# First GEMM of blocks 2 to 5: three products by one level as PSUM chains, four by two levels that add to them; the second GEMM in another order

## The chip, the cores and the metric

One Trainium2 chip, one of its cores. The time is device microseconds for one launch. The kernel before takes 632.58 us (median of 3 runs, 631.98 to 633.35). The engines are TensorE (PE in the profile, PEld its weight loads), VectorE (DVE), ScalarE (ACT), GpSimd (POOL) and SyncE (SP), which here issues every transfer.

## The reference

Retention (a linear recurrence over 768 steps with a decay for each head), then a two-layer network with ELU between the layers:

```python
B, H, S, D = 4, 8, 768, 64        # 3072 tokens, 512 features
for t in range(S):
    state = gamma[None, :, None, None] * state + np.einsum('bhd,bhe->bhde', k[:, :, t], v[:, :, t])
    y[:, :, t] = scale * np.einsum('bhd,bhde->bhe', q[:, :, t], state)
x = y.transpose(0, 2, 1, 3).reshape(B * S, H * D)
h = x @ w_in                      # 3072x512 @ 512x2048
g = np.where(h > 0.0, h, np.exp(np.minimum(h, 0.0)) - 1.0)
out = g @ w_out                   # 3072x2048 @ 2048x512
```

## The kernel before, in words

Tokens go in six blocks of 512 (`tb` 0 to 5). A block has a first GEMM (x by w_in), an ELU on its 128x8192 result, and a second GEMM (g by w_out). Meanwhile the retention of the next block is computed in pieces (`retention_step`: scores, states, three steps of outputs). Everything is fp32, and everything is kept in the order in which the program issues it: each engine works through its own queue in that order, and waits where an operand isn't there yet.

Both GEMMs are multiplied by Strassen's scheme in Winograd's form: seven products M1 to M7 of quarter matrices in place of eight, with sums before (on the operands) and after (on the results). "Two levels" applies the scheme again inside one of the seven. In blocks 2 to 5:

- First GEMM. M2 and M3 go by two levels (`first_twice`, seven inner products of four matmuls with 128 columns each, L885). The other five go by one level (`first_rest`, L931: for each of four row groups `n` four matmuls with 256 columns). Products that are to be added on the TensorE share a PSUM bank: M1, M6 and M5 of a row group run into the same bank `qa`, M7 and M4 into `qd`, and between them ScalarE copies what stands there so far (`kept`, L704). VectorE adds the pieces that stand in different banks (L899, L939).
- ELU (`elu`, L486): ScalarE computes relu and exp (L491, L492), VectorE closes with one scalar_tensor_tensor (L495), which is queued in a list `later` and issued some steps further on. A block has 16 such tiles of 128x512. They are spread over the first GEMM and the start of the second. After a row group's last tile VectorE forms T3 = C22 - C12 and T1 = C12 - C11 (L944).
- Second GEMM (`second_twice`): seven products in the order `ORDER2` = 1, 2, 6, 7, 5, 3, 4, each by two levels: seven inner products of four 128-column matmuls (L973), 49 in all. For each of the seven VectorE forms four sums of its input (`input_parts`, L847), and twice a new input in C11 (`next_input`, L787). Inner products use three PSUM tags: `pa` (two banks), `pb`, `pd` (one bank each). p1, p6, p5, p3 of a product run into one `pa` bank, p7 and p4 into `pd`, p2 into `pb`; the next of the seven begins before the last two inner products of the one before are done.
- Weights of inner products come from DRAM: `fetch_small` (L809) issues a 256 KB load into a ring of 11 slots (`wq`) whenever a slot comes free.
- Retention: the chunk of q, k and v is loaded (`load`, L110, 1 MB, four for a block), GpSimd scales v by a decay (`scale_v`, L286), and VectorE multiplies the outputs, on their way from PSUM, by powers of the decay in `etab` (L398).
- Blocks 0 and 1 go by one level in the first GEMM (`first`, L758). The second GEMM of block 1 already goes by `second_twice`, and during block 1 the inner sums of w_in for M2 and M3 are formed by VectorE and written to DRAM (`combine_small`, L833; the writes are L657).

Of the kernel before, what the change touches and what calls it, by code (L numbers as in the profile page):

```python
# [18 lines left out]
def kernel(  # L19
# [71 lines left out]
    gq["T1"] = gq["C12"]  # L91
# [197 lines left out]

    rows = lambda n: slice(n * D, (n + 1) * D)  # L290
# [87 lines left out]
    def outputs(tb, pp):  # L378
# [18 lines left out]
        for sub in range(2):  # L397
            nc.vector.tensor_tensor(  # L398
                out=place_of(x_of(tb)[:, :, 2 * pp * C : 2 * (pp + 1) * C])[:, :, :, sub, :], in0=y[sub],
                in1=place_of(powers[:, :, i * C : (i + 2) * C])[:, :, :, sub, :], op=ALU.mult,  # L400
            )
# [344 lines left out]
    def first(n):  # L746
# [18 lines left out]
        def use(name, h):  # L765
            flat = lambda x: x.rearrange("p a b -> p (a b)")
            elu(flat(mine(name)), flat(h))
            if name == "C12":

                sub = lambda o, x, y: nc.vector.tensor_tensor(out=o, in0=x, in1=y, op=ALU.subtract)  # L770
                later.append(lambda: sub(mine("T3"), mine("C22"), mine("C12")))
                later.append(lambda: sub(mine("T1"), mine("C12"), mine("C11")))
# [5 lines left out]
    ORDER2 = [1, 2, 6, 7, 5, 3, 4]  # L778

    INPUT2 = {1: "C11", 2: "C21", 3: "C22", 4: "C11", 5: "T1", 6: "C11", 7: "T3"}  # L780

    def next_input(j):

        x, op = {2: ("T3", ALU.add), 6: ("C21", ALU.subtract)}[j]
        for n in range(NQ):
            q = slice(2 * n, 2 * n + 2)
            nc.vector.tensor_tensor(out=gq["C11"][:, q], in0=gq[x][:, q], in1=gq["C11"][:, q], op=op)  # L787
# [4 lines left out]
    TWICE = [2, 3]  # L792
    SMALL = {5: 0, 6: 1, 7: 2, 3: 3}
    small_w, to_fetch, before = [], [], []
    for tb in range(1, NTB):
        for j in TWICE if tb > 1 else []:
            m1, m2, *mine = [(tb, 0, j, k) for k in (1, 2, 6, 7, 5, 4, 3)]
            to_fetch += [m1] + before[:1] + [m2] + mine[:2] + before[1:] + mine[2:3]
            before = mine[3:]
        to_fetch, before = to_fetch + before, []  # L800
        for j in ORDER2:
            last = (4, 3) if j == 4 and tb == NTB - 1 else (3, 4)
            mine = [(tb, 1, j, k) for k in (1, 2, 6, 7, 5) + last]
            to_fetch += mine[:2] + before + mine[2:5]
            before = mine[5:]
        to_fetch, before = to_fetch + before, []
# [19 lines left out]
    W_IN = {2: w_a_[:, :, :, 1], 3: w_s_[:, :, 2]}  # L826

    def combine_small(j):

        t = stage.tile([P, 4, 4, P], FP32, name="wi", tag="stage")  # L830
# [25 lines left out]
    def combine_x_twice():  # L856

        t = tpool.tile([P, 4, 2, 2, P], FP32, name="ts", tag="ts")
        b = [xb[:, 2 + k].rearrange("p (h t c) -> p t h c", h=2, t=2)[:, u] for k in range(2) for u in range(2)]
        for _ in quarters_of_input(t[:, :, 0], *b):  # L860
            pass
        for n, j in enumerate(TWICE):
            b11, b12, b21, b22 = (x[:, n] for x in b)
            s1, s2, s3, s4 = (t[:, k, 0, n] for k in range(4))
            xs[j] = {1: b11, 2: b21, 3: b22, 4: s4, 5: s1, 6: s2, 7: s3}


    PLACE = {2: "C11", 3: "C12"}

    def first_twice(tb, j):  # L870

        dst = PLACE[j]
        place = lambda name, r, t: gq[name][:, 4 * r : 4 * r + 4, P * t : P * t + P]
        full = lambda t: t.rearrange("p a (b c) -> p (a b) c", c=P)
# [17 lines left out]
        def lift(ps, o=None):  # L892
            if o is None:
                o = full(mpool.tile([P, 2, TH], FP32, name="m", tag="m"))
            nc.scalar.copy(o, ps)
            return o

        def plus(r, t, ps, m):
            nc.vector.tensor_tensor(out=place(dst, r, t), in0=ps, in1=m, op=ALU.add)  # L899

        pa = full(bank("a"))
        product(1, pa, True)
        m1 = lift(pa)
        yield
        pb = full(bank("b"))
        product(2, pb, True)
        plus(0, 0, pb, m1)
        product(6, pa, False)
        u2 = lift(pa)
        pd = full(bank("d"))  # L910
        product(7, pd, True)
        m7 = lift(pd)
        yield
        product(5, pa, False)
        plus(1, 1, pa, m7)
        yield
        product(4, pd, False)
        plus(1, 0, pd, u2)
        yield
        product(3, pa, False)  # L920
        lift(pa, place(dst, 0, 1))

    def first_rest(n, j, ps):
# [3 lines left out]
            4: (w_b[n][:, :, 1], xt[3]), 7: (w_s[n][:, 1], xt[2]),  # L927
        }[j]
        for fi in range(2):
            for j2 in range(2):  # L930
                nc.tensor.matmul(  # L931
                    ps[:, fi, :], lhsT=w[:, fi, j2, :], rhs=x[:, j2, :],
                    start=(j in (1, 7) and fi == 0 and j2 == 0), stop=(j2 == 1), skip_group_check=True,
                )

    def first_end(n, name, ps, x=None):

        g = gq[name][:, 2 * n : 2 * n + 2, :]
        nc.vector.tensor_tensor(out=g, in0=ps, in1=g if x is None else x, op=ALU.add)  # L939
        g = g.rearrange("p a b -> p (a b)")  # L940

        def combine():
            mine = lambda x: gq[x][:, 2 * n : 2 * n + 2, :].rearrange("p a b -> p (a b)")
            sub = lambda o, x, y: nc.vector.tensor_tensor(out=o, in0=x, in1=y, op=ALU.subtract)  # L944
            sub(mine("T3"), mine("C22"), mine("C12"))
            if n < NQ - 1:
                sub(mine("T1"), mine("C12"), mine("C11"))
            else:
                later.append(lambda: sub(mine("T1"), mine("C12"), mine("C11")))

        return lambda: elu(g, g, 3, combine if name == "C22" else None)

    def second_twice(tb, behind_last):
        quarter = lambda x, r, t: x[:, 4 * r : 4 * r + 4, P * t : P * t + P]
        ts, kept2 = {}, {}

        def inputs(j):
            for _ in input_parts(j):
                pass

        def input_parts(j):
            x, t = gq[INPUT2[j]], tpool.tile([P, 4, 4, P], FP32, name="ts", tag="ts")
            b11, b12, b21, b22 = (quarter(x, a, b) for a in range(2) for b in range(2))
            for n, _ in enumerate(quarters_of_input(t, b11, b12, b21, b22)):
                if n == 1:
                    yield
            ts[j] = {1: b11, 2: b21, 3: b22, 4: t[:, 3], 5: t[:, 0], 6: t[:, 1], 7: t[:, 2]}
# [15 lines left out]

        def add(o, x, y):
            nc.vector.tensor_tensor(out=o, in0=x, in1=y, op=ALU.add)  # L985
# [64 lines left out]
        def sum_up(j, m):  # L1050

            kept2[j] = m
            if j == 2:
                add(m, kept2[1], m)
                store("C11", m)
            elif j == 6:
                add(m, kept2[1], m)
            elif j == 5:
                add(m, kept2[6], m)
                h = hpool.tile([P, 512], FP32, name="h", tag="h")  # L1060
# [3 lines left out]
            elif j == 3:  # L1064
                add(m, kept2[5], m)
                store("C12", m)
# [4 lines left out]
        for _ in input_parts(1):  # L1071
            yield "input"
        yield "inputs"
        before = iter(())
        for at, j in enumerate(ORDER2):
# [3 lines left out]
            if j == 1:  # L1079
                yield "tail"  # L1080
            for _ in before:
                pass
            if at:
                yield "first"
            if j == 2:
                flush()
                next_input(2)
            if j == 5:
                next_input(6)
            if j == 1:  # L1090

                next(cur)
                yield "elu"
                next(cur)
            parts = input_parts(ORDER2[at + 1]) if at + 1 < 7 else iter(())
            if j in (2, 5):

                next(parts)
            else:
                for _ in parts:  # L1100
                    pass
            if at == 6:
                behind_last()
            if j != 1:
                next(cur)
                yield "middle"
                next(cur)
            for _ in parts:
                pass
            before = cur  # L1110
            yield j
        for _ in before:
            yield "rest"
# [189 lines left out]
    some(smalls[2], 1)  # L1303
    for n in range(NQ):
# [8 lines left out]
        if n in (1, 2):  # L1313
            some(smalls[n + 1], 1)
        elif n == 3:
            scale_v(2 * CPB, True)
        for _ in tail:
            pass
        for at, s in enumerate(cur):
            next(sides[n], None)  # L1320
# [8 lines left out]
        for _ in sides[n]:  # L1329
            pass  # L1330
        tail = cur
# [10 lines left out]
    sec = second_twice(1, combine_x_twice)  # L1342
    for _ in range(3):
        next(sec)
    next(tail)
    next(tail)
    next(sec)
    for _ in tail:
        pass
    flush()  # L1350
    step, VISITS = 0, [(0, "end"), (2, "middle"), (3, "first"), (4, "end"), (5, "end")]
    for s in sec:
        if s == "first":
            step += 1
        at = (step, s if s in ("first", "middle") else "end")
        if at in VISITS:
            retention_step(2, VISITS.index(at))
        if s == ORDER2[-1]:
            break
    tail = sec  # L1360


    for tb in range(2, NTB):
        more = tb + 1 < NTB
        qa, qd, u2, end = {}, {}, {}, None

        def rest(n, j):
# [143 lines left out]
```

## Time and profile before

| | us |
|---|---|
| median of 3 runs | 632.58 (631.98 to 633.35) |
| profiled execution, span | 631.6 |
| block 2, from its first matmul | 234.2 |
| block 3: first GEMM and retention from 334.12 to 385.75, the rest to 433.50 | 51.6 + 47.8 |
| PE busy / DVE busy / ACT busy / POOL busy | 623.8 / 482.1 / 255.3 / 22.1 |
| mean DMA rate over the span | 214 GB/s |

The span is the time from the first to the last instruction of the one execution that was profiled. "Busy" of PE counts a matmul from its start to its modelled end, and those overlap by some 0.17 us, so what a group of matmuls costs is read from the starts of the groups that follow each other. In a timeline line the first number is the start, the second the duration, and the bracket at the end is the idle time of the engine before it, with what ended that.

### The profile page before, as it was taken

How to read it: one execution, taken by the hardware profiler on the slowest of the kernel's cores; microseconds unless marked ns; L12 is line 12 of the kernel's file. 1: busy time of each engine (PE TensorE's matmuls, PEld its weight loads, DVE VectorE, ACT ScalarE, POOL GpSimd, SP SyncE). 2: the span in 40 equal slices, each digit the busy share in tenths (PEclk: the TensorE clock that was granted, in tenths of full speed). 3: DMA queues.
4: the chain of work that ended last, by engine and by line, in shares of the span. 5: the costliest groups of instructions: out<-in, count | busy, mean ns of one | idle time of the engine just before them, and what ended most of it. 6: DMA issues, size and time to landing. Idle time of an engine off the chain costs nothing.

```text
span 631.6 us, 16140 instructions
## 1 busy us (share of the span) xinstructions
PE 623.8 (99%) x6678; PEld 560.5 (89%) x6678; DVE 482.1 (76%) x882; ACT 255.3 (40%) x476; POOL 22.1 (4%) x30
## 2 busy tenths in 40 slices
PE   8999999999999999999999999999999999999997
PEld 6864578888899999888999989999989999988997
DVE  6688789989799665799585589777489877558975
ACT  6798646025541114553112646112465211366311
POOL 1021000000000000200000100000110000000000
PEclk9999999999999999999999999999999999999999
DMA  8698669699288788306888702889810698700794
GB/s 329 260 416 295 186 202 268 196 272 319 113 266 257 234 258 315 141 2 199 257 258 296 278 2 71 268 280 289 317 64 16 220 310 252 207 17 4 239 309 151
DMA packets 75897, 136.32 MB, mean 216 GB/s; under 512 B 6320, under 2 KB 31792, under 8 KB 70832
## 3 DMA queue, kind: packets, MB, share of 16 engines
q1 hardware_dynamic: 75824, 135.29, 64.9%
q8 instruction: 53, 0.87, 0.5%
q14 instruction: 20, 0.16, 0.1%
HBM read 114.03 MB, written 21.23 MB: 214 GB/s over the span
## 4 chain that ended last, share of the span: by engine, by line
PE 98%; DVE 0%; issue 0%; ACT 0%
PE pa L973 20%; PE pa L931 10%; PE pd L973 10%; PE pb L973 5%; PE pa L885 5%; PE pb L931 4%; PE pa L758 4%; PE pa L535 3%; PE qa L931 3%; PE x L625 3%; PE pd L885 2%; PE qd L931 2%; PE pd L931 2%; PE pd L758 2%; PE pa L625 2%; PE kv L352 2%
## 5 line engine op out<-in xcount | busy, mean ns | idle before, releaser
L981 ACT COPY ms<-pa 128x128 f32<-128x128 f32 x104 | 27.6, 265 | 148.2 <-PE pa L973 148.2
L973 PE MATMUL pa<-ts,wq 128*128 128x128 f32 x560 | 74.2, 275 | 0.0
L973 PE MATMUL pd<-ts,wq 128*128 128x128 f32 x552 | 73.5, 276 | 0.0
L973 PEld LDWEIGHTS pa<-ts,wq 128*128 128x128 f32 x560 | 68.5, 192 | 0.4
L973 PEld LDWEIGHTS pd<-ts,wq 128*128 128x128 f32 x552 | 67.1, 192 | 0.6 <-DVE res L985 0.2
L973 PE MATMUL pa<-gC,wq 128*128 128x128 f32 x480 | 64.6, 278 | 0.0
L492 ACT ACTIVATE r<-r 128x512 f32<-128x512 f32 x96 | 60.5, 631 | 3.1
L973 PEld LDWEIGHTS pa<-gC,wq 128*128 128x128 f32 x480 | 59.0, 192 | 1.3
L491 ACT ACTIVATE r<-gC 128x512 f32<-128x512 f32 x64 | 39.9, 624 | 31.9 <-DVE gC L939 31.9
L985 DVE TENSOR_TENSOR res<-pd,ms 128x128 f32<-128x128 f32 x68 | 19.5, 287 | 39.6 <-PE pd L973 38.4
L495 DVE SCALAR_TENSOR_TENSOR gC<-r,gC 128x512 f32<-128x512 f32 x64 | 42.6, 697 | 0.7 <-ACT r L492 0.7
L847 DVE TENSOR_TENSOR ts<-gC,ts 128x512 f32<-128x512 f32 x60 | 41.3, 688 | 1.0
L847 DVE TENSOR_TENSOR ts<-gC 128x512 f32<-128x512 f32 x60 | 41.0, 683 | 0.0
L286 POOL TENSOR_TENSOR chunk<-chunk,vf 128x512 f32<-128x512 f32 x16 | 19.4, 1212 | 429.6 <-DMA chunk<-in_qkv_dram 429.6
L973 PE MATMUL pb<-gC,wq 128*128 128x128 f32 x240 | 31.7, 275 | 0.0
L1006 ACT COPY res<-pa 128x128 f32<-128x128 f32 x34 | 9.0, 265 | 55.1 <-PE pa L973 55.1
L973 PEld LDWEIGHTS pb<-gC,wq 128*128 128x128 f32 x240 | 29.2, 192 | 0.0
L704 ACT COPY m<-pa 128x512 f32<-128x512 f32 x24 | 14.0, 582 | 33.0 <-PE pa L758 18.7
L939 DVE TENSOR_TENSOR gC<-qa,gC 128x512 f32<-128x512 f32 x8 | 5.5, 692 | 25.0 <-PE qa L931 18.3
L931 PE MATMUL pa<-xt,w_s 128*128 128x256 f32 x96 | 23.0, 382 | 0.0
L931 PE MATMUL pa<-xt,w_b 128*128 128x256 f32 x96 | 23.0, 382 | 0.0
L931 PE MATMUL pa<-xb,w_a 128*128 128x256 f32 x96 | 22.7, 379 | 0.0
(262 smaller groups left out, 1247.4 us busy)
## 6 DMA issues: line engine op xcount, KB each, us to landing
wq<-scratch_dram SPq DMA_DIRECT2D x277, 256.0 KB, 4.4
chunk<-in_qkv_dram SPq DMA_DIRECT2D x22, 1024.0 KB, 8.7
wraw<-in_w_dram SPq DMA_DIRECT2D x15, 1024.0 KB, 6.0
out_dram<-res SPq DMA_DIRECT2D x14, 256.0 KB, 4.1
scratch_dram<-gT SPq DMA_DIRECT2D x12, 256.0 KB, 4.3
scratch_dram<-m SPq DMA_DIRECT2D x12, 192.0 KB, 6.1
scratch_dram<-so SPq DMA_DIRECT2D x4, 512.0 KB, 4.7
scratch_dram<-wi SPq DMA_DIRECT2D x2, 1024.0 KB, 6.5
```

What stands on the lines that cost most here:

```text
L286: eng.tensor_tensor(out=v, in0=v, in1=vf[:, i].unsqueeze(2).to_broadcast([C, H, D]), op=ALU.mult)
L491: nc.scalar.activation(e, h, AF.Relu, scale=-1.0)
L492: nc.scalar.activation(e, e, AF.Exp, scale=-1.0)
L495: nc.vector.scalar_tensor_tensor(g, e, -1.0, h, ALU.add, ALU.max)
L625: nc.tensor.matmul(X[j][:, d, :], lhsT=w[j][:, d * P : d * P + P], rhs=x[j], start=(n == 0 and d == 0), stop=at_end, skip_group_check=True,)
L758: nc.tensor.matmul(ps[:, fi, :], lhsT=w[:, fi, j2, :], rhs=x[:, j2, :], start=(begin and fi == 0 and j2 == 0), stop=(j2 == 1), skip_group_ ...
L847: sub = lambda o, x, y: nc.vector.tensor_tensor(out=o, in0=x, in1=y, op=ALU.subtract)
L885: nc.tensor.matmul(ps[:, f, :], lhsT=lhs[f], rhs=xs[j][k], start=(begin and f == 0), stop=True, skip_group_check=True,)
L931: nc.tensor.matmul(ps[:, fi, :], lhsT=w[:, fi, j2, :], rhs=x[:, j2, :], start=(j in (1, 7) and fi == 0 and j2 == 0), stop=(j2 == 1), skip_ ...
L973: nc.tensor.matmul(ps, lhsT=w[:, f, :], rhs=ts[j][k][:, f, :], start=(begin and f == 0), stop=(f == 3), skip_group_check=True,)
L981: nc.scalar.copy(m, ps)
L985: nc.vector.tensor_tensor(out=o, in0=x, in1=y, op=ALU.add)
```

## The change

In blocks 2 to 5 the first GEMM is rearranged. For each row group M1, M6 and M5 run as a chain in one PSUM bank (`first_one`), and after each of the three ScalarE copies the running sum into the place where it will be needed: M1 into C11, M1+M6 into C21, M1+M6+M5 into C12. Then M7, M4, M2 and M3, in this order (`UNITS`), go by two levels (`unit`). The results of a unit's inner products are added by VectorE to what stands in its destinations (M7 has two destinations, the others one). Inside a unit, ScalarE copies p1 from `pa` to `pb`, where p2 is then accumulated on it. The four ELU tiles of a unit's result are issued during the next unit, the last four during the start of the second GEMM.

The second GEMM's order becomes 2, 1, 3, 7, 6, 5, 4 (1, 2, 3, ... in block 1), with the inputs formed by `form`: T3 = C12 - C11, C12 = C22 - C12, C11 = C22 - T3, C21 = C21 - C11. T1 goes.

Besides: VectorE forms the sums of w_in for M7 and M4 too, during block 1's second GEMM, in the storage of `xt_`, and two more 1 MB writes put them into DRAM. The inputs of all four units are summed at the start of a block (`combine_x_twice`). For blocks 2 to 5 the powers of the decay are multiplied into q by GpSimd (`scale_q`, in place), from a table that ScalarE builds with eight exps during the first row group of block 1; the outputs then leave PSUM by a ScalarE copy. The four chunks of the next block are loaded together at a block's start. The order of each engine's instructions in the built program follows the calls below.

```diff
+    def scale_q(m):
+        i = chunks[m][1]
+        q = raw[m][0][:, 0]
+        nc.gpsimd.tensor_tensor(out=q, in0=q, in1=qtab[:, :, i * C : (i + 1) * C], op=ALU.mult)
...
+            if tb > 1:
+                nc.scalar.copy(to, y[sub])
...
-    ORDER2 = [1, 2, 6, 7, 5, 3, 4]
+    ORDER2 = {tb: [1, 2, 3, 7, 6, 5, 4] if tb == 1 else [2, 1, 3, 7, 6, 5, 4] for tb in range(1, NTB)}
+    UNITS = {7: [("C22", "C12"), ("C21", "C21")], 4: [("C21", "C21")], 2: [("C11", "C11")], 3: [("C12", "C12")]}
...
+        def sums(r, t, ps):
+            for dst, z in dsts:
+                add(place(dst, r, t), ps, place(z, r, t))
...
+        product(1, pa, True)
+        nc.scalar.copy(pb, pa)
+        yield
+        product(2, pb, False)
+        sums(0, 0, pb)
+        yield
+        product(6, pa, False)
+        u2 = new(mpool, "m")
+        nc.scalar.copy(u2, pa)
+        if len(dsts) == 1:
+            add(u2, u2, place(dsts[0][1], 1, 0))
+        yield
+        pd = full(bank("d"))
+        product(7, pd, True)
+        m7 = new(hpool, "h")
+        if len(dsts) == 1:
+            add(m7, pd, place(dsts[0][1], 1, 1))
+        else:
+            nc.scalar.copy(m7, pd)
+        product(5, pa, False)
+        if len(dsts) == 1:
+            add(place(dsts[0][0], 1, 1), pa, m7)
+        else:
+            add(m7, pa, m7)
+            sums(1, 1, m7)
+        yield
+        product(3, pa, False)
+        sums(0, 1, pa)
+        yield
+        product(4, pd, False)
+        if len(dsts) == 1:
+            add(place(dsts[0][0], 1, 0), pd, u2)
+        else:
+            add(u2, pd, u2)
+            sums(1, 0, u2)
...
+        for n in range(CPB if more else 0):
+            load((tb + 1) * CPB + n)
+            scale_q((tb + 1) * CPB + n)
+            scale_v((tb + 1) * CPB + n)
+        first_one(0, 1, qa[0])
...
+        for n, j in ((0, 6), (1, 6), (0, 5), (1, 5), (2, 1), (3, 1), (2, 6), (3, 6)):
+            first_one(n, j, qa[n])
...
+        cur = unit(tb, FIRST2[0])
+        next(cur)
+        first_one(2, 5, qa[2])
+        first_one(3, 5, qa[3])
+        if more:
+            retention_step(tb + 1, 0)
+        for _ in range(3):
+            next(cur)
+        tail = cur
+        for at, j in enumerate(FIRST2[1:]):
+            was = FIRST2[at]
+            if at == 1 and more:
+                retention_step(tb + 1, 1)
+            cur = unit(tb, j)
+            next(cur)
+            elu_of(was, 0, 0)
+            elu_of(was, 1, 1)
+            next(tail)
+            next(tail, None)
+            elu_of(was, 0, 1)
+            next(cur)
+            pop(2)
+            next(cur)
+            elu_of(was, 1, 0)
+            pop()
+            next(cur)
+            pop()
+            if at == 2:
+                for w in inputs_of(2, ts):
+                    w()
+            tail = cur
```

`first_one(n, j, ps)` is `first_rest` for j = 1, 6, 5 followed by the ScalarE copy; `pop` issues the oldest ELU closing from `later`; `inputs_of(2, ts)` are the four input sums of the second GEMM's product 2.

## The prediction

> **What bounds the kernel now.** I read the page's totals, then the chain of waits, then the table by windows for block 3, then the timelines of the engines inside it.
>
> ```profile
> span 631.6 us, 16140 instructions
> PE 623.8 (99%) x6678; PEld 560.5 (89%) x6678; DVE 482.1 (76%) x882; ACT 255.3 (40%) x476; POOL 22.1 (4%) x30
> ...
> PE 98%; DVE 0%; issue 0%; ACT 0%
> ...
> 334.12:385.75 51.63, 51.63 (x523) 47.01 (x522) 34.59 (x57) 25.54 (x45) 4.17 (x4) 1.00 0.46 164
> 385.75:433.50 47.75, 47.75 (x617) 46.89 (x616) 38.46 (x78) 10.46 (x32) 0.00 (x0) 1.00 0.78 244
> ```
>
> The chain is TensorE alone. In block 3 (334.12 to 433.50, 99.4 us) PE never pauses, at full granted clock (1.00). So removed matmuls count in full, as long as nobody makes PE wait. The columns of the two windows are length, busy time of PE, PEld, DVE, ACT and POOL (with instructions), PE clock, DMA share and GB/s: in the first GEMM DVE is busy 34.6 of 51.6 us and ACT 25.5, so both have room as long as their work stays spread over it.
>
> ```profile
> 337.63 1.06 PE L885 MATMUL pa<-xb,w_a 128*128 128x128 f32 x8
> 338.53 1.06 PE L885 MATMUL pb<-xb,w_a 128*128 128x128 f32 x8
> ...
> 353.69 1.89 PE L931 MATMUL qa<-xt,w_b 128*128 128x256 f32 x8
> 355.42 1.89 PE L931 MATMUL pa<-xb,w_a 128*128 128x256 f32 x8
> ```
>
> Start to start, four 128-column matmuls cost 0.893 us (7 groups from 337.63 to 343.98 take 6.35, with two of 0.94) and four 256-column ones 1.727.
>
> ```profile
> 348.37 0.69 DVE L939 TENSOR_TENSOR gC<-qa,gC 128x512 f32<-128x512 f32 x1 [1.70 <-ACT gC L895]
> 348.98 0.68 DVE L899 TENSOR_TENSOR gC<-pa,m 128x512 f32<-128x512 f32 x1
> 349.58 0.68 DVE L899 TENSOR_TENSOR gC<-pd,m 128x512 f32<-128x512 f32 x1
> ...
> 375.01 1.72 DVE L364 TENSOR_TENSOR chunk<-kv,chunk 128x256 f32<-128x256 f32 x4
> ...
> 356.41 0.63 ACT L491 ACTIVATE r<-gC 128x512 f32<-128x512 f32 x1 [1.94 <-DVE gC L939]
> 357.08 0.63 ACT L492 ACTIVATE r<-r 128x512 f32<-128x512 f32 x1
> 357.61 0.61 ACT L491 ACTIVATE r<-gC 128x512 f32<-128x512 f32 x1
> ...
> 360.80 0.59 ACT L704 COPY m<-pa 128x512 f32<-128x512 f32 x1 [0.72 <-PE pa L931]
> 361.28 0.64 ACT L491 ACTIVATE r<-gC 128x512 f32<-128x512 f32 x1
> ```
>
> These are the prices. A 128x512 DVE operation takes a slot of 0.60 (348.37, 348.98, 349.58), also from PSUM into strided places (L899); 0.72 where it needs the result just before (394.12 after 393.40); a state sum in its chain 0.44. An ELU tile takes ACT 0.66 + 0.53, a copy 0.48. From the end of a PE group (start plus slot) to its reader: 0.20 to ACT (337.63 + 0.89, copy at 338.73), 0.27 to DVE. ACT and DVE hand on some 0.03 us after their end. Nothing in the trace shows PE restarting after ACT or DVE inside a block; I take 0.10 us, bounds 0.04 and 0.30.
>
> **PE's own work.** M7 and M4 leave the one-level form: 2 x 4 groups of 1.727 = 13.82 us a block. They come back as 2 x 7 groups of 0.893 = 12.50. That is -1.31 us a block, -5.3 us in four. M1, M6, M5, M2, M3 and the second GEMM's 49 inner products keep their groups. So -5.3 us is all that there is to win, since PE has no idle time to recover.
>
> The Trainium skill, "TensorE: Matmul & The Clock Gate", Back-to-back issue gap, speaks against this: in a stream with weight loads it gives 81 ns for 128 columns and 131 for 512, so a line through them gives an estimate of 98 for 256. By that, 28 x 81 against 16 x 98 would make the two-level form 1.45 times as dear, +6.2 us a block. The rows here (0.893 against 1.727, 1.93 times) disagree, and the rows are used.
>
> **What VectorE gets.** I follow one block with its time 0 at its first matmul. Twelve one-level groups, two inner products of the block before, and unit 7's p1 fill PE to 23.4; the scores to 25.4 (2.02, as 367.60 to 369.62). Then come 7.p2, p6, p7, p5 (3.6 us) and for each of the units 4, 2, 3 seven groups in the order p1, old p3, old p4, p2, p6, p7, p5 (6.25 us); the states (2.0) stand before unit 2. In the second GEMM product 2 begins S2.p1, S2.p2, 3.p3, 3.p4, S2.p6, S2.p7. From the scores' end to S2.p7 that is 30 x 0.893 + 2.0 = 28.8 us of PE.
>
> S2.p7 overwrites `pd`, so it waits for VectorE's last add of unit 3. Before that add VectorE's queue holds 4 masks, 10 adds of unit 7 (two destinations), 3 x 6 adds of units 4, 2, 3, 12 ELU closings and 4 input sums: 48 x 0.60 = 28.8 us; 7 state sums x 0.44 = 3.1; a small add 0.2; seven places where an operation needs the one just before, 7 x 0.12 = 0.8. With hand-overs this is 33.3 us against 28.8. So PE must lose at least 4.5 us here, however the waits fall. Before, the same stretch had nothing like it, because the closings and adds were spread over the 51.6 us. In the last block (no scores, no states) the same count is 27.9 against 25.9: 2.0.
>
> The queue isn't gapless, which adds the rest. Walking the three queues with the prices above: masks hold VectorE until 28.0, so unit 7's sums start late and the lag stays. Each inner product that accumulates on a bank waits for its reader: 7.p3 0.2; 4.p5 0.3 (ScalarE's u2 copy stands behind three ELU tiles); 4.p3 0.2; 2.p7 1.3 (the state sums stand before unit 4's p4 add, which frees `pd`); 2.p5 0.3 (u2 copy); 2.p3 1.3 (p5's add stands behind m7's, two closings and u2's); 3.p3 0.3; S2.p6 0.1; S2.p7 1.8 (four input sums stand before the add); 0.1 later. Sum 6.0 us. The last block comes to 6.3 by the same walk. With restart 0.04 to 0.30 a block gives 5.8 to 7.0 (last 6.0 to 7.5). Four blocks: 3 x 6.0 + 6.3 = +24.3; floor 3 x 4.5 + 2.0 = +15.5; ceiling 3 x 7.0 + 7.5 = +28.5. The ScalarE copy from PSUM to PSUM (p1 into `pb`) has no row; bounds 0.585 (L704, PSUM to SBUF) and 0.63 (L491, SBUF to SBUF); it has 1.8 us of cover, so 0.
>
> **Block 1.** VectorE forms 8 more sums of w_in. Four stand before the masks of the scores:
>
> ```profile
> 188.96 2.48 DVE L323 TENSOR_TENSOR chunk<-sc,cmask 128x512 f32<-128x512 f32 x4
> 191.36 0.28 DVE L985 TENSOR_TENSOR res<-pb,ms 128x128 f32<-128x128 f32 x1
> 191.60 0.29 DVE L985 TENSOR_TENSOR res<-pd,ms 128x128 f32<-128x128 f32 x1
> ```
>
> The add at 191.60 frees `pd` for the group that PE starts at 192.29: 0.4 us to spare. 4 x 0.60 and two dependences, 2.65 us, push it: +2.3 us. The other four meet a stretch with an output step on PE: 0, or +1.2 if that cover fails. The eight exps (rows L254: 0.71 and 0.50 us) stand among ScalarE's copies of row group 0 and push a closing, and the add behind it that frees `pd`, by 0.7 us past need: +0.7, bounds 0 and 3. The two 1 MB writes meet transfers that are 0.75 to 0.84 busy; the ring's 11 x 0.89 us less 4.4 us of landing covers 5.4 us, about 3.5 a write: 0, bounds 0 and 3.
>
> **What costs nothing, and why.** The twelve ScalarE copies of the chains (5.8 us in 23): between a product and its continuation in the bank stands another of 1.73 us, and the copy needs 0.8. Without that cover each would cost 0.8. GpSimd's eight scalings: in block 3 three loads issued from 348.16 on were consumed by 361.64, 13.5 us, so four take some 18, the last q is scaled by 19.2, and the scores come at 23.4. Without these 4 us every late us is one of PE's, in three blocks. On SP's queue the four loads stand ahead of weight fetches, but the ring is full and isn't drawn on until 26. The input sums of units 7 and 4 (4 x 0.33) fall where VectorE is idle, and so does the saving of four output multiplications (-2.4) near a block's end. Inputs formed for the second GEMM are 16 operations before (L787, L944) and after.
>
> GpSimd's port:
>
> ```profile
> 361.64 1.04 POOL L286 TENSOR_TENSOR chunk<-chunk,vf 128x512 f32<-128x512 f32 x1 [2.16 <-DMA chunk<-in_qkv_dram]
> ...
> 361.72 1.51 DVE L944 TENSOR_TENSOR gC<-gC,gC 128x512 f32<-128x512 f32 x1
> ```
>
> One DVE sum of two SBUF operands took 1.51 instead of 0.69 beside a GpSimd operation. It costs nothing here, since GpSimd is done before the masks. The skill's "SBUF — State Buffer", Who interferes with whom, calls the shared port an exclusive lock for such pairs, so by it eight scalings would hold up VectorE by up to 8 x 0.8 = 6 us, in its idle time.
>
> **The sum.** 631.6 - 5.3 + 24.3 + 2.3 + 0.7 = 653.6 us as a span. The median of the runs stands 1.0 above this execution's span: 654.6, forecast 654.5. Its own range is 650 to 664: below, restart 0.04 (-0.9), the exps at 0 (-0.7) and the masks' push covered (-2.3); above, restart 0.30 (+4.2), the exps at 3 (+2.3), the writes at 3.
>
> **Rivals.** (1) Only VectorE's throughput counts, and its lag hides the separate waits: 631.6 + 1.0 - 5.3 + 15.5 + 0 to 3 = 643 to 646. For it: in block 3 VectorE works gaplessly from 385 to 402 and PE doesn't notice. Against: there no group waits on VectorE within 0.9 us of its producer. (2) The chunks come late: before, the first load of a block needed 7.9 us to its consumer against 4.4 for a weight; if the fourth is ready 3 us after 23.4, +9: 663. Against: the 4 us above. (3) Faster: VectorE keeps up. Place: the 48 operations between scores and S2.p7. It decides if a slot were at most 0.50, for then 24 + 4 fits in 28.8; PE's saving stays: 632.6 - 5.3 = 627.3, with block 1 up to 630. Against: every 128x512 row has 0.60. (4) The change doesn't shorten PE at all because 128-column groups lengthen to 0.94 as two did at 339.42: 28 x 0.05 more a block, 654.5 + 5.6 = 660.
>
> **Chances.** Forecast 0.62, rival 1 0.17, rivals 2 and 4 together 0.13, rival 3 0.06, between the last and the others (no change) 0.02. Predicted time 654.5. Range 642 to 664: from rival 1 to rival 2. A run can't tell less than 0.2% (1.3 us) from no change. Faster by more 0.06, within 0.02, slower by more 0.92.
>
> **What would show it.** After: PE idle of some 6 us in each of the blocks 2 to 5, between the scores and the second GEMM's first product, released by DVE adds of `pa` and `pd`; VectorE busy over 95% there; a first GEMM with no idle time before the scores; 128-column groups still at 0.893. It is wrong if PE's busy share stays at 99%, if the idle time is released by POOL or a DMA, or if it lies in the second GEMM.

## The result, and the profile after

The changed kernel takes 663.69 us (median of 4 runs, 662.38 to 665.20) against 632.43 for the kernel before: 1.049 times as long (95% interval 1.047 to 1.051). Its profiled execution has a span of 660.6 us, 29.0 more than before. One of the runs below (without the scalings of q) had its profile from a disturbed execution, so of that run only the ratio is used.

The totals and the chain of waits of the changed kernel:

```profile
span 660.6 us, 16718 instructions
PE 628.7 (95%) x6870; PEld 565.1 (86%) x6870; DVE 496.0 (75%) x914; ACT 278.9 (42%) x520; POOL 42.3 (6%) x64
...
PE 51%; DVE 22%; issue 4%; DMA 2%; ACT 1%; SPq 1%; DVEq 0%
```

TensorE was 98% of the chain and VectorE none of it; now VectorE is 22%, though it is busy 75% of the span as it was (76%). The table by windows for block 3, from its first matmul (346.98) to the scores, from there to the group S2.p7, and the rest:

```profile
346.98:371.41 24.43, 23.76 (x123) 20.81 (x121) 7.21 (x16) 7.54 (x14) 9.07 (x8) 1.00 0.72 262
371.41:407.86 36.45, 33.20 (x482) 31.55 (x481) 32.45 (x56) 23.18 (x41) 0.00 (x0) 1.00 0.46 133
407.86:452.04 44.18, 44.18 (x592) 43.62 (x593) 35.24 (x72) 10.00 (x32) 0.00 (x0) 1.00 0.79 251
```

VectorE (third busy column) has 7.2 us of work in the first 24.4 and 32.5 in the next 36.5. TensorE loses most of its time in the middle window. The timeline there, of VectorE and of the TensorE groups that stopped:

```profile
390.59 0.68 DVE L911 TENSOR_TENSOR gC<-pd,m 128x512 f32<-128x512 f32 x1
...
391.78 1.28 DVE L524 SCALAR_TENSOR_TENSOR gC<-r,gC 128x512 f32<-128x512 f32 x2
392.99 0.68 DVE L911 TENSOR_TENSOR m<-m,gC 128x512 f32<-128x512 f32 x1
393.59 0.69 DVE L524 SCALAR_TENSOR_TENSOR gC<-r,gC 128x512 f32<-128x512 f32 x1
394.19 0.68 DVE L911 TENSOR_TENSOR h<-pd,gC 128x512 f32<-128x512 f32 x1
394.98 0.69 DVE L911 TENSOR_TENSOR gC<-pa,h 128x512 f32<-128x512 f32 x1
...
407.12 0.68 DVE L911 TENSOR_TENSOR gC<-pd,m 128x512 f32<-128x512 f32 x1
```

```profile
391.32 1.16 PE L926 MATMUL pd<-ts,wq 128*128 128x128 f32 x8 [0.46 <-DVE gC L911]
...
395.72 1.16 PE L926 MATMUL pa<-xb,wq 128*128 128x128 f32 x8 [1.15 <-DVE gC L911]
...
407.86 1.16 PE L1014 MATMUL pd<-ts,wq 128*128 128x128 f32 x8 [1.43 <-DVE gC L911]
```

These are the prediction's waits 2.p7, 2.p3 and S2.p7. Before the add at 394.98, which frees `pa` for 2.p3, VectorE works without a pause through three ELU closings (L524), u2's add and m7's; the walk had the same queue there, with two closings. A visible wait understates the loss: a matmul's modelled end lies 0.17 us beyond its slot, and the group after a stop takes 1.00 instead of 0.893. So I count from start to start, less 0.893 or 1.727:

| part of the span | forecast, us | measured, us |
|---|---|---|
| TensorE's own work in blocks 2 to 5 | -5.3 | -5.3 (12 x 1.727 + 77 x 0.893 a block against 20 and 63; the slots held) |
| scores to S2.p7, four blocks | +24.3 | 6.4 + 5.7 + 6.5 + 6.5 = +25.1 |
| seam between blocks | 0 | 4 x 0.94 = +3.8 |
| block 1, first GEMM | +0.7 | 0.9 + 2.5 + 0.9 = +4.4 |
| block 1, second GEMM | +2.3 | +2.2 |
| block 0 | 0 | +0.7 (the first one-level group stood between 132.5 and 134.3 in the executions of this study) |
| small restarts elsewhere, and what stays unassigned | 0 | -1.9 |
| sum | +22.0 | +29.0 |

The row before the sum is negative mainly because the count of the stretch takes in restarts at the scores and the states that stood before, too: blocks 3 and 4 grew by 4.8 and 5.5 us, 0.6 less than their rows above give. Block 2's 6.4 holds 0.4 us in which TensorE waited for nothing that the profile shows.

The seam, block 3's beginning:

```profile
346.95 0.69 DVE L911 TENSOR_TENSOR res<-res 128x512 f32<-128x512 f32 x1
...
347.56 0.68 DVE L497 TENSOR_TENSOR xt<-xb 128x512 f32<-128x512 f32 x1
348.28 0.69 DVE L497 TENSOR_TENSOR xt<-xb,xt 128x512 f32<-128x512 f32 x1
...
349.49 0.68 DVE L497 TENSOR_TENSOR xt<-xb,xt 128x512 f32<-128x512 f32 x1
...
350.09 0.28 DVE L911 TENSOR_TENSOR res<-pd,ms 128x128 f32<-128x128 f32 x1
350.43 0.97 PEld L1014 LDWEIGHTS pd<-ts,wq 128*128 128x128 f32 x8 [0.86 <-DVE res L911]
```

Four sums of the new x (L497) stand ahead of the small add that frees `pd`. And block 1's first GEMM:

```profile
146.90 0.58 ACT L304 ACTIVATE etab<-pos,lng 128x256 f32<-128x256 f32 x1
147.39 0.56 ACT L733 COPY m<-pa 128x512 f32<-128x512 f32 x1
147.98 0.69 DVE L738 TENSOR_TENSOR h<-pb,m 128x512 f32<-128x512 f32 x1 [1.44 <-ACT m L733]
...
151.38 1.99 PE L787 MATMUL pd<-xb,w_s 128*128 128x256 f32 x8 [0.59 <-DVE h L738]
...
152.74 1.75 POOL L314 TENSOR_TENSOR chunk<-chunk,etab 128x512 f32<-128x512 f32 x1 [4.39 <-DMA chunk<-in_qkv_dram]
...
153.29 1.76 DVE L717 TENSOR_TENSOR w_s<-w_a,w_b 128x512 f32<-128x512 f32 x1
...
157.74 1.27 POOL L314 TENSOR_TENSOR chunk<-chunk,etab 128x512 f32<-128x512 f32 x1 [3.24 <-DMA chunk<-in_qkv_dram]
...
158.34 1.21 DVE L524 SCALAR_TENSOR_TENSOR gC<-r,h 128x512 f32<-128x512 f32 x1
...
160.15 1.27 POOL L314 TENSOR_TENSOR chunk<-chunk,etab 128x512 f32<-128x512 f32 x1 [1.14 <-DMA chunk<-in_qkv_dram]
...
160.19 1.77 DVE L717 TENSOR_TENSOR w_s<-w_b,w_a 128x512 f32<-128x512 f32 x1
...
166.00 1.99 PE L787 MATMUL pd<-xb,w_s 128*128 128x256 f32 x8 [2.19 <-DVE h L738]
```

Two causes follow each other here. First, VectorE waits 1.44 us for a ScalarE copy (147.39) that stands behind exps (the last at 146.90), and TensorE then stops for 0.59 us; counted from start to start, with the restart, that is 0.9. Then, while GpSimd scales q (L314), two VectorE sums take 1.76 and 1.77 us and a closing 1.21 in place of 0.69, 2.7 us more in all; that lag ends in a wait of 2.19 us, counted 2.5. The third 0.9 is a stop of 0.68 us ahead of the group at 182.55, the last but one of this GEMM.

### The profile page after: what moved, and what is told of

It reads as the page before. It is cut to its first block, busy times and chain, and to the rows that moved or that the text cites. A ratio compares the mean times of both kernels' runs of the same rounds, so it can differ in the third digit from the quotient of the medians.

```text
span 660.6 us, 16718 instructions
## 1 busy us (share of the span) xinstructions
PE 628.7 (95%) x6870; PEld 565.1 (86%) x6870; DVE 496.0 (75%) x914; ACT 278.9 (42%) x520; POOL 42.3 (6%) x64
## 4 chain that ended last, share of the span: by engine, by line
PE 51%; DVE 22%; issue 4%; DMA 2%; ACT 1%; SPq 1%; DVEq 0%
PE pa L1014 16%; PE pd L1014 9%; DVE gC L911 5%; PE pb L1014 4%; DVE gC L524 4%; PE pa L986 3%; PE pb L986 3%; PE pd L986 3%; DVE res L911 2%; PE qa L986 2%; DVE h L911 2%; PE pa L926 2%; PE pa L787 2%; DVE m L911 2%; DVE xt L497 2%
## 5 line engine op out<-in xcount | busy, mean ns | idle before, releaser
L1014 PE MATMUL pa<-ts,wq 128*128 128x128 f32 x560 | 74.5, 276 | 0.1
L1014 PEld LDWEIGHTS pa<-ts,wq 128*128 128x128 f32 x560 | 68.1, 192 | 0.8 <-issue 0.3
L349 DVE TENSOR_TENSOR chunk<-sc,cmask 128x512 f32<-128x512 f32 x22 | 13.7, 683 | 52.3 <-PE sc L338 52.3
L524 DVE SCALAR_TENSOR_TENSOR gC<-r,gC 128x512 f32<-128x512 f32 x64 | 42.1, 683 | 0.0
L314 POOL TENSOR_TENSOR chunk<-chunk,etab 128x512 f32<-128x512 f32 x16 | 20.8, 1298 | 313.3 <-DMA chunk<-in_qkv_dram 196.7
L926 PE MATMUL pa<-ts,wq 128*128 128x128 f32 x256 | 34.9, 279 | 0.2
L926 PEld LDWEIGHTS pa<-ts,wq 128*128 128x128 f32 x256 | 31.1, 191 | 1.6 <-ACT m L947 1.6
L911 DVE TENSOR_TENSOR gC<-pb,gC 128x512 f32<-128x512 f32 x20 | 13.4, 685 | 18.2 <-PE pb L926 18.2
L820 DVE TENSOR_TENSOR gC<-gC,gC 128x512 f32<-128x512 f32 x36 | 22.4, 684 | 0.0
```

Of the source, the lines that this page charges most:

```text
L314: nc.gpsimd.tensor_tensor(out=q, in0=q, in1=qtab[:, :, i * C : (i + 1) * C], op=ALU.mult)
L349: nc.vector.tensor_tensor(out=raw[tb * CPB + 2 * pp + a][0][:, 1].rearrange("p h c -> p (h c)").rearrange("p (n t) -> p n t", t=D), in0=sc ...
L524: nc.vector.scalar_tensor_tensor(g, e, -1.0, h, ALU.add, ALU.max)
L820: nc.vector.tensor_tensor(out=gq[o][:, q], in0=gq[x][:, q], in1=gq[y][:, q], op=ALU.subtract)
L926: nc.tensor.matmul(ps[:, f, :], lhsT=lhs[f], rhs=xs[j][k], start=(begin and f == 0), stop=True, skip_group_check=True,)
L1014: nc.tensor.matmul(ps, lhsT=w[:, f, :], rhs=ts[j][k][:, f, :], start=(begin and f == 0), stop=(f == 3), skip_group_check=True,)
```

## The experiments

The question was whether the loss in blocks 2 to 5 is VectorE's bunched queue, and of what the 7 us beyond the forecast are made. Each ratio is to the kernel before on the same chip; the changed kernel stands at 1.0488, and differences to it are taken from the ratios.

**Without the closings.** `elu_of` issues ScalarE's two steps only (16 closings a block go; 12 of them lay in the stretch).

```diff
-        elu(g, g, 4)
...
+        nc.scalar.activation(e, h, AF.Relu, scale=-1.0)
+        nc.scalar.activation(e, e, AF.Exp, scale=-1.0)
```

> Leaves out the closing VectorE operation of each ELU tile in blocks 2 to 5 (12 of 0.60 us a block); ScalarE's two steps stay, the output is that of a network without the ELU there. Theory (VectorE's queue is too full and in the wrong order between the scores and S2.p7): by the walk the stalls there fall from 6.0 to 2.3 us in blocks 2 to 4 and from 6.3 to 2.2 in block 5, so 663.7 - 15 = 648.6, range 646 to 651. Rival, throughput alone: 26.1 us of VectorE against 28.8 of TensorE leaves no stall at all, 663.7 - 24 = 639.5. Rival, the waits come from ScalarE, GpSimd or weights: 662 to 664.

Measured 649.33 us, ratio 1.0253 (1.0229 to 1.0278), so 14.9 us less than the changed kernel. TensorE's waits in block 2, from the table of waits between 241 and 350 us (total, times, longest):

```profile
PE pd L1017 <- DVE res L911: 1.3, 2, 0.7
PE pd L1017 <- DVE gC L911: 0.4, 1, 0.4
PE pa L926 <- ACT m L947: 0.2, 1, 0.2
```

In the changed kernel the same table has 1.4 + 1.2 + 0.6 from the adds of gC. So VectorE's work is the cause; neither of the rivals fits. 16 x 0.60 x 4 = 38 us of VectorE work went and only 15 came back: the rest of it had cost no time.

**Freeing adds first.** Same work on VectorE, other order.

```diff
-        if len(dsts) == 1:
-            add(u2, u2, place(dsts[0][1], 1, 0))
         yield
...
             add(place(dsts[0][0], 1, 1), pa, m7)
+            add(u2, u2, place(dsts[0][1], 1, 0))
...
             elu_of(was, 1, 0)
-            pop()
             next(cur)
-            pop()
+            pop(2)
             if at == 2:
-                for w in inputs_of(2, ts):
+                x2 = inputs_of(2, ts)
+                for w in x2[:2]:
                     w()
...
+                for w in x2[2:]:
+                    w()
```

> Same work, other order on VectorE in units 4, 2, 3: the adds that free a bank (m7's and p5's) stand ahead of u2's add and of the last two closings, and two of the four input sums of the second GEMM's first product stand behind unit 3's p4 add. Theory (queue full and badly ordered): by the walk 6.0 to 4.7 us a block, last 6.3 to 3.9, so 663.7 - 6.3 = 657.4, range 655.5 to 660; the floor of 4.5 stays. Rival, order alone: nearly all of the stalls go, 663.7 - 20 = 644. Rival, order is nothing: 663.7.

Measured 659.85, ratio 1.0429 (1.0411 to 1.0447): 3.7 us less, in the range, though the forecast was a gain of 6.3. The wait before 2.p3 is gone; the one before 2.p7 is there with 0.6 to 1.3 us, the one before S2.p7 fell from 1.43 to 0.87, and one of 0.44 us is new before S2.p6. That no order inside this stretch can win much is the argument of the count (33.3 us of VectorE against 28.8 of TensorE); this run, one order, agrees with it.

**Without q's scaling in block 1.**

```diff
             scale_v(2 * CPB, True)
-            for m in range(CPB):
-                scale_q(2 * CPB + m)
```

> Leaves out the four scalings of q by GpSimd in block 1 (the q of block 2 stays unscaled, its outputs change). Theory: GpSimd's operations beside VectorE's lengthen them (1.77 instead of 0.69 us at 160.19, 1.21 at 158.34), 1.6 us of the stall of 2.2 us before the group at 166.00; it falls to about 0.6 and the whole to 662.1 (661.0 to 662.8). Rival: that stall is VectorE's added sums and the exps alone, nothing changes there, 663.7.

Ratio 1.0417 (1.0399 to 1.0434), 4.5 us less (from the ends of both intervals, 2.0 to 7.0): more than the 1.6 expected. The expectation counted two lengthened VectorE operations; the third, at 153.29, makes it 2.7 us, close to the stop's 2.5, and that lies within the interval. The ratio alone doesn't say where the gain fell.

**The seam.**

```diff
-                (next_x() if more else [], []),
+                ([], next_x() if more else []),
```

The diff is that of blocks 2 to 5; block 1's list has the same edit.

> The four sums of x that open the next block stand behind the add that frees pd for the last product's p3, p4, not ahead of it. Theory: the wait of 0.83 + 0.10 us at each of the four seams goes, 663.7 - 3.7 = 660.0 (659.3 to 661). Rival: the wait only moves to the first one-level group that reads the sums (M6 of row group 0, 2.5 us later): 662 to 663.7.

Measured 660.77, ratio 1.0435 (1.0419 to 1.0451), 3.4 us less, in the range. The wait at the seam is gone in all four blocks and came back nowhere in them: the periods from block to block fell from 105.8, 105.1, 105.8 to 104.9, 104.1, 104.9.

**Powers of q a block later.**

```diff
-            if tb > 1:
+            if tb > 2:
                 nc.scalar.copy(to, y[sub])
...
-    qpowers = begin_powers_for_q()
-    next(qpowers)
...
+        if tb == 2:
+            run(begin_powers_for_q())
```

> The eight exps and the scalings of q begin one block later: block 1 has neither, block 2's outputs are multiplied by VectorE as in the kernel before, the exps stand in ScalarE's queue at block 2's start, all outputs as before. Theory (GpSimd's four scalings and the exps in block 1 lengthen and push VectorE's work there): the two stalls of 0.59 and 2.19 us ahead of the groups at 151.38 and 166.00 go, and what the run without the scalings showed beyond them: 663.7 - 4 = 659.7, range 658.5 to 661.5. Rival (VectorE's eight added sums of w_in alone make those stalls): 662.5 to 663.7.

Measured 662.01, ratio 1.0446 (1.0419 to 1.0473), 2.7 us less: between the ranges of the theory and of the rival. In the trace the two stalls of block 1 are gone, and the stretch from its first one-level group to the second GEMM's first fell from 52.8 to 49.3 us, 3.5 as expected. Some came back in block 2, where the eight exps (L303, L304) now stand in one piece ahead of ScalarE's copies:

```profile
244.95 0.71 ACT L303 ACTIVATE etab<-pos,lng 128x512 f32<-128x512 f32 x1
245.57 0.59 ACT L304 ACTIVATE etab<-pos,lng 128x256 f32<-128x256 f32 x1
246.06 0.57 ACT L990 COPY gC<-pb 128x512 f32<-128x512 f32 x1
246.53 0.58 ACT L990 COPY gC<-qa 128x512 f32<-128x512 f32 x1
246.68 1.99 PE L986 MATMUL pb<-xt,w_s 128*128 128x256 f32 x8 [0.73 <-ACT gC L990]
```

In the profiled execution block 3 lost another 1.44 us to a wait for nothing that the profile shows, and the last block some 1.7 to a lower clock (last section). Exps and scalings moved together here; the trace of the changed kernel parts their shares of the 3.5 us in block 1, 0.9 and 2.5.

**Block 1's order.**

```diff
-    next(tail)
-    next(tail)
     tail = second_twice(1, ts, work_of_second, visit_of_second)
...
-            (i(2), small_part(7)), (i(3), []), ...
+            (i(2), []), (i(3), small_part(7)), ...
```

> Block 1 alone: the second GEMM's first two groups stand ahead of the last two one-level groups again, as in the kernel before, and the four sums of w_in for M7 stand one product later, behind the masks. Theory: the stall of 0.68 us ahead of the group at 182.55 (and its restart, 0.1) and the one of 1.79 at 199.21 (restart 0.1) go: 663.7 - 2.7 = 661.0, range 660.2 to 662. Rival: the sums push the next product's adds instead and the second stall comes back there: 662.5 to 663.

Measured 664.26, ratio 1.0485 (1.0461 to 1.0510): no gain, so by the time a miss. In its trace both stalls are gone (the 0.68; the 1.79, counted 1.95 from start to start, became 0.8 at a wait for a ScalarE copy), but the granted clock was 0.66 from 165 to 170 us, where one group took 3.45 instead of 1.83 us, it fell in the same way at 595, and a wait in this block for nothing that the profile shows took 2.12 us instead of 1.28. As a time this run is inconclusive; the next pair holds the same edit.

**The spread order.** Blocks 2 to 5 with the same operations, in an order found by walking the queues of the prediction with its prices over many orders. M1 of all row groups comes first, so unit 2 (which needs nothing but C11) can start at once, and the other eight one-level groups, on which VectorE has nothing to do, stand between the units' products. `f06` is M6 of row group 0, `2p75` unit 2's p7 and p5, `E2:00` ScalarE's part of an ELU tile, `S` a closing, `I10` an input sum, `Qa1` the first two inner products of the second GEMM's product 1:

```diff
+        "f01 tail 2p1 f11 t0 f21 2p2 2p6 f31 t1 E2:00 S 2p75 f06 f16 2p3 4p1 au2 E2:01 2p4 f26 4p2 f36 4p6 "
+        "f05 4p75 au4 E2:11 S E2:10 S 7p1 f15 S 7p2 I10 4p3 E21:00 4p4 I11 sc0 S E7:00 I12 S f35 f25 7p6 I13 "
+        "sc1 st0 7p75 3p1 7p3 E7:01 7p4 3p2 3p6 E7:10 au3 E7:11 3p75 S S S Qa1 3p3 E21:11 E21:10 3p4 S Qb1 S "
...
```

> Blocks 2 to 5 with the same operations in another order (units 2, 4, 7, 3; the one-level groups spread among the units; scores and states in halves; second GEMM's first products 1, 3, 2; the next block's sums behind the add at the seam), so that VectorE works evenly instead of idling for 17 us and then falling behind. Block 1 as in the changed kernel. Theory (the loss in blocks 2 to 5 is VectorE's bunched queue, TensorE's own work is 1.3 us a block shorter): by the walk stalls of 0.5 instead of 6.0 us a block and none at the seam, 663.7 - 4 x 6.4 = 638.1, range 636 to 642; block period about 99.4 us against 105.5. Rival (TensorE's work isn't shorter, groups lengthen): period 100.7 or more, over 643. Rival (the waits return at weights or chunks, which are now drawn earlier): over 645, released by DMA or POOL.

Measured 641.36, ratio 1.0135 (1.0119 to 1.0151), 22.3 us less. (In this run and the next the outputs aren't the reference's: as read in the last section, unit 2's first quarter has M1 in 128 of its 512 columns only; all the work is done.) Block periods 99.7, 100.9 and 99.8; the 100.9 holds 0.6 us of waits for nothing that the profile shows. In the blocks TensorE waits for no weight or chunk, and for VectorE 0.12 us once a block; the only longer wait for VectorE is one of 1.01 us at the kernel's end (0.65 in the changed kernel). Both rivals are out.

> The spread order of blocks 2 to 5 and both edits of block 1 together (exps and scalings of q one block later, with the exps spread among the one-level groups of block 2; the second GEMM's first groups and the sums of w_in for M7 as in the run on block 1's order). Theory: 638.1 - 3.5 - 2.2 = 632.4, range 630 to 635.5: what the change saves on TensorE about pays for what stays in block 1, so no more than 0.5% either way against the kernel before. Rival (block 1's stalls come back in block 2, as the exps did): 635 to 638. Rival (faster): under 630 if block 1 costs nothing any more.

Measured 635.04, ratio 1.0033 (1.0021 to 1.0045): 6.5 us less than the run before it, for the edits of block 1 (5.7 expected). That is in the range and at the edge of the first rival's; but in its trace block 2 has no stop over 0.12 us, while block 3 holds 1.6 us of waits for nothing that the profile shows, so that rival isn't what came.

**Towards the best order.** In the next run the scores' halves stand together (`sc0 sc1`), unit 2's M1 is copied into a bank of the retention's pool, and w_in's sums are written in four pieces. The rest of its order differs from the run before as well, so what it gains isn't the gain of these three edits alone. By the same reading unit 4's first quarter lost M1 in it, where unit 2's had before.

> As the run with both edits, with three more: unit 2's M1 goes into a bank of the retention's pool, whose 512 columns were all written before (in the two runs before it, the bank that the second GEMM had begun with 128 columns took M1 from ScalarE and unit 2's first quarter lost M1 in three of four column groups); the halves of the scores stand together again; the sums of w_in for M7 and M4 are written in four pieces each. Theory: 635.0 - 0.4 a block for the scores - 0.8 for the wait for a weight in block 1 = 632.8, range 631 to 635, within 0.3% of the kernel before: TensorE's 1.3 us a block is all but spent on restarts and on block 1. Rival (faster): under 630.5, if the switches between kinds of groups cost more than 0.2 us each. Rival (slower): over 636, if the fetches or the bank's release now wait.

Measured 631.60, ratio 0.9975 (0.9963 to 0.9987). Then nothing is added in a bank that was begun with 128 columns:

```diff
             product(1, t["a"], True)
-            nc.scalar.copy(t["b"], t["a"])
+            if j == 2:
+                t["m1"] = new(mpool, "m")
+            nc.scalar.copy(t["m1"] if j == 2 else t["b"], t["a"])
...
-            product(2, t["b"], False)
-            sums(0, 0, t["b"])
+            product(2, t["b"], j == 2)
+            if j == 2:
+                add(t["m1"], t["m1"], place("C11", 0, 0))
+                add(place("C11", 0, 0), t["b"], t["m1"])
```

> As the run before it, but unit 2 joins M1 and M2 on VectorE (M1 copied to SBUF, one more add of 0.60 us a block) and its M2 begins the bank with all 512 columns, so that no unit adds onto a bank that was begun with 128; the outputs are the reference's. Theory: the added operation falls where VectorE idles, so 631.6 as that run, range 630 to 633.5, 0.1 to 0.4% under the kernel before. Rival: unit 2's first sum now comes later and holds bank b for unit 4: one wait of 0.5 us a block, 633.5.

Measured 632.00, ratio 0.9984 (0.9972 to 0.9995).

> The same with another of the orders that the walk finds equal (0.5 us of stalls a block): 631.6, range 630 to 633.5. If the two differ by over 1.5 us, the walk misses something that decides between them.

Measured 631.17, ratio 0.9971 (0.9953 to 0.9989), a little faster than the kernel before; the two orders differ by 0.8 us, and the outputs of both are the reference's. Its totals, chain, and block 3 by windows (to the scores, to the second GEMM, the rest):

```profile
span 628.6 us, 16734 instructions
PE 621.1 (99%) x6870; PEld 563.6 (90%) x6870; DVE 500.6 (80%) x922; ACT 275.2 (44%) x516; POOL 40.0 (6%) x60
...
PE 94%; DVE 3%; DMA 1%; ACT 1%; issue 1%; SPq 0%; DVEq 0%
```

```profile
333.57:371.00 37.43, 37.43 (x249) 35.01 (x248) 24.86 (x40) 17.39 (x31) 9.77 (x8) 1.00 0.67 238
371.00:386.20 15.20, 15.20 (x275) 14.54 (x275) 14.05 (x24) 8.90 (x16) 0.00 (x0) 1.00 0.45 128
386.20:432.90 46.70, 46.70 (x679) 45.88 (x676) 39.43 (x82) 14.09 (x39) 0.00 (x0) 1.00 0.79 248
```

VectorE now does 24.9 us in the first 37.4 where it did 7.2 in 24.4, though its work is 3.4 us a block more (78.3 against 74.9), and TensorE never stops in this block.

## Why the prediction was right, and where it was short

- **TensorE's own work, -1.31 us a block**: right. The slots of 0.893 and 1.727 held beside every wait, so the fourth rival (longer 128-column groups) is out. The estimate set against it, worked out from the figures of the Trainium skill's "TensorE: Matmul & The Clock Gate", Back-to-back issue gap, would have made the work 6.2 us a block longer; the runs don't agree with it here. With the last spread order a block takes 99.3 us (99.35, 99.33, then 99.72) against 100.3 before (334.12 to 434.40; the 433.50 and 99.4 given ahead leave out the block's last group, and block 2's first matmul stands at 232.35, not 234.2). So 0.9 of the 1.3 arrive in block 3; of the rest, 0.2 are groups beyond their slots (1.45 us a block, before 1.25) and 0.2 the states in two halves (1.08 + 1.09 in place of 2.01).
- **The stretch from the scores to S2.p7, +24.3**: right in size (25.1), place and releaser. The stop before 2.p3 was forecast at 1.3 and measured at 1.31 (block 3); S2.p7 1.8 and 1.66; 2.p7 1.3 and 0.62 to 1.35; last block 6.3 and 6.5, a third of it in one stop of 2.06 us before 4.p3. That VectorE's work in the stretch is the cause is shown by the run without the closings and by the spread order, which keeps the work and moves it out of the stretch. The prediction's ten waits add up to 5.9, not 6.0; that changes nothing.
- **Rival 1 (throughput alone)**: out; 639.5 would have followed without the closings, against 649.33 (its row isn't quite so, either: before, VectorE idles 0.21 us at 389.46). **Rival 2 (late chunks)**: out. Its number, 663, is the time that came, by another way: no stop in block 3's scores is released by POOL or a DMA, and GpSimd was done with the last scaling of v at 367.1 us, 4.3 before the scores (the last q was scaled 19.1 us into the block, forecast 19.2). **Rival 3 (faster)**: its condition, a slot of 0.50, never came; the adds stayed at 0.60.
- **"The saving of four output multiplications falls near a block's end" and the second GEMM's inputs as equal before and after**: the step that missed 3.8 us. The amount of work was counted and its new place was not: the sums of the next x moved ahead of an add that frees a bank, in an idle stretch of VectorE that has one deadline in it. The seam run shows it.
- **"The eight exps ... +0.7, bounds 0 and 3"**: right (0.9, and at the add that frees `pd`). **GpSimd's port "costs nothing here, since GpSimd is done before the masks"**: the step that missed 2.5 us. The port was weighed in block 3 alone. In block 1 three of the four scalings of q met a VectorE without idle time and added 1.07, 0.52 and 1.08 us to its operations. The exclusive lock that the prediction cited ("SBUF — State Buffer", Who interferes with whom) is in line with that; what was wrong is that it would fall into idle time. Exps and scalings together cost 3.5 us in block 1, by the run that moved them. To this comes a stop of 0.68 us (counted 0.9) at the end of block 1's first GEMM, which the prediction didn't walk: two groups that had covered the reuse of `pa` stood behind it. It is gone in the run that puts them back.
- **The small sums ahead of the masks, +2.3**: right (the stop at 199.21 was 1.95 from start to start, and the group behind it 0.1 longer).
- **Span to median**: 1.0 was taken over from before; the median lies 3.1 above this profiled execution, as that was the shortest of four (660.6; the others 661.8 to 663.4). A run's time is some 1.8 above its own span (662.38 and 660.6), so the 631.6 before belong to the longest of its three runs (633.35). The 2.1 us between 1.0 and 3.1 come from which executions were profiled.

Forecast 654.5, measured 663.69: sign, mechanism and largest term right, the time 9.2 us short, at the range's upper end. That the range still held it is in part luck: its top stood for late chunks, long restarts and slow writes, none of which came, and it took up the seam and the scalings, which had been put at nothing.

## What to carry to other kernels

An engine that is 75% busy can still set the time, if its work is bunched: count its operations between two fixed points of the critical engine, and look for what could be done in the stretch where it idles. Walk the queue at every place to which an operation moves, not only where the change is meant to act: a moved operation delays what frees a bank behind it, even next to an idle stretch. Products that leave nothing to the lagging engine are the cover to spread among those that do.

## What the runs showed of the hardware that was not expected

- A stop of TensorE costs more than its record shows: 0.67 us visible at the seam was 0.83, and the group after it took 1.00 in place of 0.893, 0.94 in all. From VectorE's end to TensorE's start it took 0.05 to 0.06 us (394.98 + 0.69 to 395.72, 350.09 + 0.28 to 350.43). A switch from GEMM groups to scores or outputs, and back, cost 0.09 and 0.10 even without a wait.
- Where a unit added onto what ScalarE had copied into a PSUM bank that the second GEMM had begun with 128 columns, the outputs weren't the reference's (three spread runs). They are in the changed kernel, where one-level groups write all 512 columns of the bank between, and in the last two orders, where unit 2's product begins the bank itself. My reading is that the copy was kept in the 128 columns and overwritten in the other 384; no run here shows the columns. The Trainium skill's "PSUM — Partial Sum Buffer", The four PSUM rules, has the rule: a write by ScalarE leaves the accumulator's written marks as they are, a matmul that begins a bank clears them for the whole bank, and a later one adds only where they are set. The runs agree with it as far as they go.
- Waits of TensorE for nothing that the profile shows move from place to place with the program: 1.25 us in block 2 before, 1.28 in block 1 after, 2.12 with block 1's order, 0.20 in the last run. Differences of one us between two programs can come from there; what they are stays open.
- In the traces read here, from 30 us on, TensorE has eleven stops of over 2 us. Behind five of them the granted clock fell to 0.5 for some 3.4 us: at 167.46 after 2.51 us (the seam's run), 595.14 after 2.05 (powers later), 165.75 after 2.45 and 595.58 after 2.05 (block 1's order), 166.04 after 2.50 (the first spread run). The other six, of 2.05 to 2.61 us, show no fall, and neither does any stop of 1.79 us or less. One fall costs some 1.7 us (an estimate: 3.4 us at half the clock), so a long stop can cost more than its length in one execution and not in the next.
